# V fetched in 64 KB rows into one 8 MB slot, PV of a pair of units in its own loop pass, and one merge for all groups at the end

## The chip, the cores and the metric

One core of one Trainium2 chip. The metric is the device time of the core in microseconds (us); a run is one execution. Engines are called as in the profile: PE (matmul), PEld (PE's weight loads), DVE, ACT, POOL (GpSimd) and SP (which issues nearly all DMA). A "DMA engine" is one of the 16 that move the core's data.

## The reference

One token is decoded: layer norm, a grouped-query attention over a long cache, and beside it a small dense layer with GELU.

```
B, Sq, D = 1, 1, 512;  Hq, Hkv, Sk, Dh = 32, 8, 65536, 128     # bf16
xn = layernorm(x)
q  = (xn @ wq) per head                       # 32 heads, 4 per kv group
p  = softmax(q @ k_cache^T * Dh**-0.5)
attention = (p @ v_cache) @ wo
dense     = gelu(xn @ w1 + b1) @ w2 + b2      # F = 1792
out = x + attention + dense
```

K and V are 128 MB each (8 groups x 65536 keys x 128 x 2 bytes). Sizes of transfers and slots are in powers of two; the profile's own MB are millions of bytes. In those, K and V are 268.4 MB, and with the weights 280.5 MB have to be read for a result of 1 KB.

## The kernel before

The cache is cut into 32 units of 16384 keys; 4 units make a group. A unit's K and V are 4 MB each. On one partition a unit is 128 keys of 256 bytes in a row: 32 KB. For each unit PE transposes K (128 transposes, drained by DVE and ACT), multiplies it with q (scores), DVE and ACT make the stable exponentials P, and PE multiplies V with P (PV). SBUF has four slots of 4 MB, two for K and two for V, and the loop runs over pairs of units. PV of a unit runs two units late, so the first pass has a dummy PV and the last two PVs come after the loop. Every group is merged (weighted by its units' maxima) inside the loop.

```python
    chunks = [("K", 0), ("K", 1)]                 # order of the DMA queue
    for u in range(2, NU):
        chunks += [("V", u - 2), ("K", u)]
    chunks += [("V", NU - 2), ("V", NU - 1), ("W", 0)]
# ... [cut] ...
            src = cache[0, g, c * CKEYS:(c + 1) * CKEYS, :].rearrange("(p t) d -> p t d", p=128)
            sch.dma(SP, lambda b=b, src=src: sp.dma_start(out=slot[b], in_=src), csem[b], writes=[f"slot{b}"])
# ... [cut] ...
    def half(i, b):                               # one unit; a loop pass is half(i, 0), half(i, 1)
        u = 2 * i + b
        # ... [cut: weigh_2, weigh_3 of the last group when it has ended] ...
        pv(u - 2)
        transposes(b, 0)
        stats_1()
        transposes(b, 1)
        stats_2(u - 1)
        # ... [cut] ...
        transposes(b, 2)
        scores(b, 0)
        transposes(b, 3)
        done_chunk("K", u)                        # the slot is free: SP may issue the next K
        scores(b, 1)
        # ... [cut: weigh_1, total] ...
        scores(b, 2)
        scores(b, 3)
# ... [cut] ...  after the loop:
    stats_1(); stats_2(L); pv(L - 1); weigh_1(); total(); weigh_2()
    # ... [cut] ...
    pv(L)
    weigh_3(oT_last)
    # ... [cut: 136 small matmuls with wo, output] ...
```

The output weights wo ("W", 4 MB) come last, into the K slots.

Of the kernel before, what the change touches and what calls it, by code (L numbers as in the profile page):

```python
# [237 lines left out]
def bass_parallel_sum__gqa_block_cached__dense_activation_gelu__decode_kernel(  # L238
# [14 lines left out]
    DH = 128  # L253
# [33 lines left out]
    SP = sch.add_engine("sp", "sp")  # L287

# [6 lines left out]
    def sb(name, shape, dt):  # L295
# [14 lines left out]
    qT_bf = sb("qT_bf", [128, H], BF)  # L310
# [13 lines left out]
            for i in range(NSLOT)]  # L324
    wq_sb = kv[:, NK * TPD * DH:NK * TPD * DH + KT * H * DH].rearrange("p (kt n) -> p kt n", kt=KT)
# [11 lines left out]

    pmax = sb("pmax", [128, HPG], F32)
    gmax4 = sb("gmax4", [HPG, 1], F32)
    diag4 = sb("diag4", [HPG, HPG], F32)  # L340
    negm = sb("negm", [128, GW], F32)
    sums = sb("sums", [128, GW], F32)
    sums_cur = sb("sums_cur", [128, GW], F32)
    o_all = sb("o_all", [128, GW], F32)
    coef = sb("coef", [128, GW], F32)
    wtot = sb("wtot", [128, GW], F32)
    o_c = sb("o_c", [128, GW], F32)
    nmin = sb("nmin", [128, HPG], F32)
    rden = sb("rden", [128, HPG], F32)
    o_sum = sb("o_sum", [128, HPG], F32)  # L350
    oT_all = sb("oT_all", [128, G * HPG], BF)
    oT_last = sb("oT_last", [128, HPG], BF)
    oX_bf = sb("oX_bf", [128, HPG, GE], BF)
    spare = sb("spare", [128, 1], F32)
# [13 lines left out]
    csem = [sch.dsem(f"csem{i}") for i in range(NSLOT)]  # L368
    sem_x = sch.dsem("dx")
    sem_misc = sch.dsem("dmisc")  # L370
    sem_w1 = sch.dsem("dw1")
    wsem = [sch.dsem(f"wsem{i}") for i in range(4)]
    sem_out = sch.dsem("dout")

    for t, res, v in ((pmax, "pmax", 0.0), (negm, None, 0.0), (sums, None, 1.0), (sums_cur, "sums_cur", 1.0),
                      (o_all, None, 0.0), (coef, "coef", 1.0)):
        names = [res] if res else {
            id(negm): [f"negm{c}" for c in range(CPG)], id(sums): [f"sums{a}" for a in range(GW)],
            id(o_all): [f"o{c}" for c in range(CPG)]}[id(t)]
        sch.op(POOL, lambda t=t, v=v: pool.memset(t[:, :], v), writes=names)  # L380
# [12 lines left out]
    w_end = w2_at + FC * D  # L393
    if w_end < NSLOT * TPD * DH:
        sch.op(POOL, lambda: pool.memset(kv[:, w_end:NSLOT * TPD * DH], 0.0), writes=["w_pad"])
    for k in range(2):
        sch.op(POOL, lambda k=k: pool.memset(P_bf[k][:, :], 0.0), writes=[f"P{k}_{j}" for j in range(HPG)])


    chunks = [("K", 0), ("K", 1)]  # L400
    for u in range(2, NU):
        chunks += [("V", u - 2), ("K", u)]
    chunks += [("V", NU - 2), ("V", NU - 1), ("W", 0)]
    next_chunk = [0]
    slot_free = [True, True, False, False]

    def slot_of(kind, u):
        return u % 2 + (NK if kind == "V" else 0)

    def issue_chunks():  # L410
        while next_chunk[0] < len(chunks):
            kind, u = chunks[next_chunk[0]]
            if kind == "W":
                if not (slot_free[0] and slot_free[1]):
                    return
                dma_wo()
                next_chunk[0] += 1
                return
            b = slot_of(kind, u)
            if not slot_free[b]:  # L420
                return
            slot_free[b] = False
            g, c = divmod(u, CPG)
            cache = A_k_cache if kind == "K" else A_v_cache
            src = cache[0, g, c * CKEYS:(c + 1) * CKEYS, :].rearrange("(p t) d -> p t d", p=128)
            sch.dma(SP, lambda b=b, src=src: sp.dma_start(out=slot[b], in_=src), csem[b], writes=[f"slot{b}"])
            next_chunk[0] += 1

    def done_chunk(kind, u):
        slot_free[slot_of(kind, u)] = True  # L430
        issue_chunks()
# [10 lines left out]
    def dma_wq():  # L442
        sch.dma(SP, lambda: sp.dma_start(out=wq_sb, in_=A_wq.rearrange("(p kt) n -> p kt n", kt=KT)),  # L443
                csem[NK], writes=[f"slot{NK}"])

    def dma_w12():
# [4 lines left out]
                csem[NK + 1], writes=[f"slot{NK + 1}"])  # L451
# [58 lines left out]
    def qproj():  # L510
        for b in range(2):
            for kt in range(KT):
                for j in range(4):
                    c0 = (b * 4 + j) * 512
                    row_mm(pss[b][32 * j:32 * j + 1, :], xnT_bf[:, kt:kt + 1], wq_sb[:, kt, c0:c0 + 512],
                           [f"slot{NK}", "xnT"], f"pss{b}", kt == 0, kt == KT - 1, kt == KT - 1 and j == 3)
# [8 lines left out]
        sch.op(DVE, lambda: dve.tensor_copy(out=qT_bf[:, :], in_=pA[:, PA_Q:PA_Q + H]), reads=["pA"], writes=["qT"])  # L525

    def ffn():
        for s in range(FC // 2):
            b, j = divmod(s, 4)
            for kt in range(KT):  # L530
                row_mm(pO[32 * j:32 * j + 1, b * 256:(b + 1) * 256], xnT_bf[:, kt:kt + 1],
                       w1_sb[:, kt, :, 2 * s:2 * s + 2], ["w1", "xnT"], "pO", kt == 0, kt == KT - 1,
# [22 lines left out]
        for fc in range(FC):  # L555
            row_mm(pO[32 * (fc % 4):32 * (fc % 4) + 1, :], gT_bf[:, fc:fc + 1], w2_sb[:, fc, :],
                   [f"slot{NK + 1}", "gT"], "pO", fc < 4, fc >= FC - 4 and fc % 4 != 3, False)
# [45 lines left out]
    group = [None]  # L603

    def load_q(u):
        def copy():
            cols = slice(0, HPG) if group[0] is None else bass.ds(group[0] * HPG, HPG)
            return dve.tensor_copy(out=q_cur[:, :], in_=qT_bf[:, cols])

        sch.op(DVE, copy, reads=["qT"], writes=["q_cur"])  # L610
# [11 lines left out]
    def stats_2(u):  # L622
        k, c = u % 2, u % CPG
        us = slice(c * HPG, (c + 1) * HPG)
# [5 lines left out]
               reads=["pA"], writes=[f"negm{c}"])  # L630
        src = pss[k][:, 0:CW].rearrange("p (t j) -> p t j", j=HPG)
        for j in range(HPG):
            at = c * HPG + j
# [5 lines left out]
                reads=[f"negm{c}", f"pss{k}"],  # L639
                writes=[f"P{k}_{j}", f"sums{at}"],  # L640
            )


    def pv(u):
        k, b = u % 2, slot_of("V", u)
        for t in range(TPD):
            sch.op(
                PE,
                lambda k=k, b=b, t=t: pe.matmul(  # L649
                    pO[:, 0:HPG], lhsT=slot[b][:, t, :], rhs=P_v[k][:, t, :],  # L650
                    start=t == 0, stop=t == TPD - 1),
                reads=[f"slot{b}"] + (["w_pad"] if u == -1 and "w_pad" in sch.last_write else []) + [f"P{k}_{j}" for j in range(HPG)], writes=["pO"],
                publish=t == TPD - 1,
            )
        done_chunk("V", u)
        c = u % CPG
        us = slice(c * HPG, (c + 1) * HPG)
        sch.op(DVE, lambda us=us: dve.tensor_copy(out=o_all[:, us], in_=pO[:, 0:HPG]),  # L658
               reads=["pO"], writes=[f"o{c}"])


    negm_v, coef_v = (t[:, :].rearrange("p (h j) -> p h j", j=HPG) for t in (negm, coef))
    negm_r, wtot_r, oc_r = (t[:, :].rearrange("p (h j) -> p j h", j=HPG) for t in (negm, wtot, o_c))

    def weigh_1():
        neg = [f"negm{c}" for c in range(CPG)]
        sch.op(DVE, lambda: dve.tensor_reduce(out=nmin[:, :], in_=negm_r, axis=AX.X, op=ALU.min),
               reads=neg, writes=["nmin"])
        sch.op(DVE, lambda: dve.tensor_tensor(
            out=coef_v, in0=nmin[:, :].unsqueeze(1).to_broadcast([128, CPG, HPG]), in1=negm_v,  # L670
            op=ALU.subtract), reads=["nmin"] + neg, writes=["coef"])
        sch.op(DVE, lambda: dve.tensor_copy(out=sums_cur[:, :], in_=sums[:, :]),  # L672
               reads=[f"sums{at}" for at in range(GW)], writes=["sums_cur"])
        sch.op(ACT, lambda: act.activation(out=coef[:, :], in_=coef[:, :], func=ACTF.Exp),
               reads=["coef"], writes=["coef"])

    def total():
        sch.op(PE, lambda: pe.matmul(pA[:, PA_SUM:PA_SUM + GW], lhsT=ones_f[:, :], rhs=sums_cur[:, :],  # L678
                                     start=True, stop=True), reads=["ones_f", "sums_cur"], writes=["pA"])

    def weigh_2():
        sch.op(DVE, lambda: dve.tensor_tensor(out=wtot[:, :], in0=coef[:, :], in1=pA[:, PA_SUM:PA_SUM + GW],
                                              op=ALU.mult), reads=["coef", "pA"], writes=["wtot"])
        sch.op(DVE, lambda: dve.tensor_reduce(out=rden[:, :], in_=wtot_r, axis=AX.X, op=ALU.add),
               reads=["wtot"], writes=["rden"])
        sch.op(DVE, lambda: dve.reciprocal(out=rden[:, :], in_=rden[:, :]), reads=["rden"], writes=["rden"])

    def weigh_3(out=None):
        sch.op(DVE, lambda: dve.tensor_tensor(out=o_c[:, :], in0=o_all[:, :], in1=coef[:, :], op=ALU.mult),
               reads=["coef"] + [f"o{c}" for c in range(CPG)], writes=["o_c"])  # L690
        sch.op(DVE, lambda: dve.tensor_reduce(out=o_sum[:, :], in_=oc_r, axis=AX.X, op=ALU.add),
               reads=["o_c"], writes=["o_sum"])

        def scale():
            dst = out[:, :] if out is not None else oT_all[:, bass.ds(group[0] * HPG, HPG)]
            return dve.tensor_tensor(out=dst, in0=o_sum[:, :], in1=rden[:, :], op=ALU.mult)

        sch.op(DVE, scale, reads=["o_sum", "rden"], writes=["oT" if out is None else "oL"])


    def half(i, b):
        u = 2 * i + b
        odd = i % 2
        if b == 0:
            if odd:
                weigh_2()
                weigh_3()
            else:
                DVE.pending += 6
# [136 lines left out]
```

## Time and profile before

| | before |
|---|---|
| time, median (3 runs) | 661.83 us (661.66 to 662.32) |
| span of the profiled run | 659.8 us |
| HBM read | 280.50 MB, 425 GB/s over the span |
| PE busy | 567.6 us (86%) |

Lines of the profile's page of the kernel before: busy time by engine, the 40 slices, the DMA part, and the chain of work that ended last. The digits are tenths of a slice; GB/s is what the DMA engines moved in each slice.

```profile
span 659.8 us, 28552 instructions
PE 567.6 (86%) x12957; PEld 530.4 (80%) x12957; DVE 279.4 (42%) x616; ACT 244.9 (37%) x470; POOL 4.2 (1%) x19
...
PEclk9686777777788866778876678876767887676785
DMA  9999999999999999999999999999999999999996
GB/s 369 441 426 433 420 436 423 443 425 435 431 427 439 429 435 428 429 435 425 441 427 433 431 427 437 431 435 429 429 437 425 441 425 433 433 425 437 431 428 251
...
q1 hardware_dynamic: 11128, 280.50, 99.1%
q8 instruction: 10, 0.16, 0.1%
...
DMA 59%; PE 38%; issue 1%; DVE 1%; SPq 0%; DVEq 0%
```

The DMA row has nines to the last slice, and the load queue (q1) has transfers under way for 99.1% of 16 engines' span. PE is busy too, but the next two views show it waiting. The names in them: kv holds the four slots, pst PE's transposes, pss its scores (at the end, the products with wo), pO its PV products. First who waited for whom on PE in the kernel before (total us, times, longest), then the end of its timeline (start, length, engine, line, what, and in brackets the idle before it).

```profile
PE pst L569 <- DMA kv<-in_A_k_cache_dram: 49.3, 25, 3.0
PE pO L649 <- DVE pmax L597: 11.8, 15, 0.8
...
PE pss L773 <- DMA kv<-in_A_wo_dram: 2.1, 1, 2.1
```

```profile
625.46 3.59 PE L569 MATMUL pst<-ident_bf,kv 128*128 128x128 bf16 x32 [2.54 <-DMA kv<-in_A_k_cache_dram]
...
655.36 1.61 PE L773 MATMUL pss<-kv,oX_bf 128*1 128x128 bf16 x48 [2.06 <-DMA kv<-in_A_wo_dram]
656.66 0.74 PE L773 MATMUL pss<-kv,oT_last 128*1 128x128 bf16 x16
```

PE waits for K at nearly every unit, and at the very end for the last weights. So the kernel is bound by its DMA. How long DMA takes can be read one level lower, from the records of single rows in the trace: one 32 KB row takes 1215 ns (median) on its DMA engine and the next row follows within nanoseconds.

### The profile page before, as it was taken

What the parts mean: (1) busy time and instruction counts of PE and PEld (TensorE: products, weight loads), DVE (VectorE), ACT (ScalarE), POOL (GpSimd) and SP (SyncE); (2) the same over time, 40 slices, a digit from 0 to 9 for tenths busy, and PEclk for the clock granted to TensorE, in tenths of its full rate; (3) what the DMA queues carried; (4) which work ended last, traced back from release to release, by engine and by line L of the source; (5) the groups of instructions that cost most, each with busy time, mean ns of one, the idle gap of its engine ahead of it and who ended that gap; (6) DMA issues with size and microseconds to landing.
All of it is one profiled execution on the core that took longest, in us unless ns stands there. A gap on an engine that the chain in (4) does not pass through costs nothing.

```text
span 659.8 us, 28552 instructions
## 1 busy us (share of the span) xinstructions
PE 567.6 (86%) x12957; PEld 530.4 (80%) x12957; DVE 279.4 (42%) x616; ACT 244.9 (37%) x470; POOL 4.2 (1%) x19
## 2 busy tenths in 40 slices
PE   2597899999889988889898888988888998888896
PEld 0387899999888877878887788978878897787885
DVE  5153444454345443444444334544433444443341
ACT  0143344444344432334443233443323444332350
POOL 2000000000000000000000000000000000000000
PEclk9686777777788866778876678876767887676785
DMA  9999999999999999999999999999999999999996
GB/s 369 441 426 433 420 436 423 443 425 435 431 427 439 429 435 428 429 435 425 441 427 433 431 427 437 431 435 429 429 437 425 441 425 433 433 425 437 431 428 251
DMA packets 11288, 280.69 MB, mean 425 GB/s; under 512 B 1290, under 2 KB 1804, under 8 KB 2700
## 3 DMA queue, kind: packets, MB, share of 16 engines
q1 hardware_dynamic: 11128, 280.50, 99.1%
q8 instruction: 10, 0.16, 0.1%
q10 hardware_dynamic: 148, 0.01, 0.0%
q14 instruction: 2, 0.02, 0.0%
HBM read 280.50 MB, written 0.00 MB: 425 GB/s over the span
## 4 chain that ended last, share of the span: by engine, by line
DMA 59%; PE 38%; issue 1%; DVE 1%; SPq 0%; DVEq 0%
DMA kv<-in_A_k_cache_dram 55%; PE pst L569 27%; DMA kv<-in_A_wo_dram 5%; PE pss L589 5%; PE pO L649 4%; PE pA L614 1%; PE pA L625 1%; DVE pmax L597 0%; PE pss L773 0%; DVE kt_ring L577 0%; PE pA L678 0%; SPq L450 0%; SPq L459 0%; SPq L447 0%; SPq L443 0%
## 5 line engine op out<-in xcount | busy, mean ns | idle before, releaser
L569 PE MATMUL pst<-ident_bf,kv 128*128 128x128 bf16 x4096 | 313.3, 245 | 49.6 <-DMA kv<-in_A_k_cache_dram 49.3
L569 PEld LDWEIGHTS pst<-ident_bf,kv 128*128 128x128 bf16 x4096 | 284.5, 112 | 68.6 <-DMA kv<-in_A_k_cache_dram 51.5
L579 ACT ACTIVATE kt_ring<-pst 128x1024 bf16<-128x1024 bf16 x192 | 198.2, 1032 | 376.0 <-PE pst L569 373.3
L577 DVE COPY kt_ring<-pst 128x1024 bf16<-128x1024 bf16 x320 | 211.8, 688 | 178.9 <-PE pst L569 178.3
L649 PE MATMUL pO<-P_bf,kv 128*128 128x4 bf16 x4352 | 120.7, 166 | 17.0 <-DVE pmax L597 11.8
L649 PEld LDWEIGHTS pO<-P_bf,kv 128*128 128x128 bf16 x4352 | 118.0, 103 | 19.1 <-DVE pmax L597 13.1
L589 PE MATMUL pss<-q_cur,kt_ring 128*128 128x4 bf16 x4096 | 114.1, 164 | 2.4 <-issue 2.4
L589 PEld LDWEIGHTS pss<-q_cur,kt_ring 128*128 128x128 bf16 x4096 | 111.8, 96 | 2.5 <-issue 2.5
L636 ACT ACTIVATE P_bf<-pss,negm 128x128 bf16<-128x128 f32 x132 | 52.5, 553 | 4.0 <-DVE negm L628 4.0
L597 DVE TENSOR_REDUCE pmax<-pss 128x4 f32<-128x512 f32 x32 | 22.1, 691 | 68.7 <-PE pss L589 68.7
L658 DVE COPY o_all<-pO 128x4 f32<-128x4 f32 x34 | 5.5, 161 | 104.9 <-PE pO L649 104.9
L636 ACT ACTIVATION_READ_ACCUMULATOR P_bf<-pss,negm 128x1 f32 x132 | 37.4, 283 | 0.0
L614 PE MATMUL pA<-ident_f,pmax 128*4 128x128 f32 x66 | 16.2, 339 | 0.8 <-DVE pmax L597 0.8
L625 PE MATMUL pA<-diag,ones_f 4*128 4x4 f32 x66 | 12.8, 261 | 0.6 <-DVE diag L618 0.6
L625 PEld LDWEIGHTS pA<-diag,ones_f 4*128 4x128 f32 x66 | 9.8, 186 | 4.2 <-DVE diag L618 0.9
L500 PE MATMUL pA<-ones_bf,xn_row 1*128 1x1 bf16 x4 | 0.3, 174 | 10.5 <-DVE xn_row L496 10.5
L616 DVE TENSOR_REDUCE gmax<-pA 4x1 f32<-4x128 f32 x33 | 8.9, 269 | 0.5 <-PE pA L614 0.5
L500 PEld LDWEIGHTS pA<-ones_bf,xn_row 1*128 1x128 bf16 x4 | 0.2, 116 | 10.5 <-DVE xn_row L496 10.5
L614 PEld LDWEIGHTS pA<-ident_f,pmax 128*4 128x4 f32 x66 | 3.0, 84 | 6.4 <-DVE kt_ring L577 4.5
L678 PE MATMUL pA<-sums_cur,ones_f 128*128 128x16 f32 x34 | 6.8, 275 | 1.3 <-DVE sums_cur L672 0.6
L618 DVE TENSOR_SCALAR diag<-ident_f,gmax 4x4 f32<-4x4 f32 x33 | 7.2, 217 | 1.2
L678 PEld LDWEIGHTS pA<-sums_cur,ones_f 128*128 128x128 f32 x34 | 5.3, 195 | 2.2 <-DVE sums_cur L672 2.2
(82 smaller groups left out, 66.3 us busy)
## 6 DMA issues: line engine op xcount, KB each, us to landing
kv<-in_A_k_cache_dram SPq DMA_DIRECT2D x32, 4096.0 KB, 27.5
kv<-in_A_v_cache_dram SPq DMA_DIRECT2D x32, 4096.0 KB, 30.7
kv<-in_A_wq_dram SPq DMA_DIRECT2D x1, 4096.0 KB, 12.3
kv<-in_B_w_dram SPq DMA_DIRECT2D x2, 1792.0 KB, 18.0
kv<-in_A_wo_dram SPq DMA_DIRECT2D x1, 2048.0 KB, 27.5
kv<-in_A_wo_dram SPq DMA_DIRECT2D x1, 1536.0 KB, 31.5
kv<-in_A_wo_dram SPq DMA_DIRECT2D x1, 384.0 KB, 19.5
kv<-in_A_wo_dram SPq DMA_DIRECT2D x1, 128.0 KB, 19.4
```

The source lines that it names most:

```text
L569: lambda tb=tb, at=at, b=b, tt=s * TPB + t: pe.transpose(pst[tb][:, at * 128:(at + 1) * 128], slot[b][:, tt, :], ident_bf[:, :]),
L577: e, fn = DVE, lambda tb=tb, dst=dst: dve.tensor_copy(out=dst, in_=pst[tb][:, :])
L579: e, fn = ACT, lambda tb=tb, dst=dst: act.activation(out=dst, in_=pst[tb][:, :], func=ACTF.Copy)
L589: lambda k=k, kb=kb, at=at, t=t: pe.matmul(pss[k][:, at:at + HPG], lhsT=kt_ring[:, kb * BCOL + t * 128:kb * BCOL + (t + 1) * 128], rhs=q_c ...
L597: lambda k=k: dve.tensor_reduce(out=pmax[:, :], in_=pss[k][:, 0:CW].rearrange("p (t j) -> p j t", j=HPG), axis=AX.X, op=ALU.max),
L614: sch.op(PE, lambda: pe.matmul(pA[0:HPG, PA_ST:PA_ST + 128], lhsT=pmax[:, 0:HPG], rhs=ident_f[:, :], start=True, stop=True), reads=["pmax" ...
L616: sch.op(DVE, lambda: dve.tensor_reduce(out=gmax4[:, :], in_=pA[0:HPG, PA_ST:PA_ST + 128], axis=AX.X, op=ALU.max), reads=["pA"], writes=[" ...
L618: sch.op(DVE, lambda: dve.tensor_scalar(out=diag4[:, :], in0=ident_f[0:HPG, 0:HPG], scalar1=gmax4[0:HPG, 0:1], scalar2=None, op0=ALU.mult) ...
L625: sch.op(PE, lambda: pe.matmul(pA[:, PA_SB:PA_SB + HPG], lhsT=ones_f[0:HPG, 0:128], rhs=diag4[0:HPG, 0:HPG], start=True, stop=True), reads ...
L636: lambda k=k, at=at, j=j, src=src: act.activation(out=P_v[k][:, :, j], in_=src[:, :, j], func=ACTF.Exp, bias=negm[:, at:at + 1], scale=1.0 ...
L649: lambda k=k, b=b, t=t: pe.matmul(pO[:, 0:HPG], lhsT=slot[b][:, t, :], rhs=P_v[k][:, t, :], start=t == 0, stop=t == TPD - 1),
L678: sch.op(PE, lambda: pe.matmul(pA[:, PA_SUM:PA_SUM + GW], lhsT=ones_f[:, :], rhs=sums_cur[:, :], start=True, stop=True), reads=["ones_f", ...
```

## The change

Its intent: fewer and longer rows. Two neighbouring units of 16384 keys lie side by side on each partition (256 keys, 64 KB), so V of a pair comes in one 8 MB transfer of 64 KB rows into one slot made of the two old V slots; K of the pair comes in two transfers of 32 KB rows that are 64 KB apart. A pair's PVs move to the end of its own loop pass, so there is no dummy first pass and no PV after the loop. The statistics of each unit are kept in columns (128 in all), and all groups are merged once in the last pass. The last V comes as two halves.

```diff
-    chunks = [("K", 0), ("K", 1)]
-    for u in range(2, NU):
-        chunks += [("V", u - 2), ("K", u)]
-    chunks += [("V", NU - 2), ("V", NU - 1), ("W", 0)]
+    chunks = []
+    for i in range(NU // 2):
+        chunks += [("K", 2 * i), ("K", 2 * i + 1), ("V", i)]
+    chunks += [("W", 0)]
 ... [cut]
+            src = cache[0, g, 2 * c * CKEYS:2 * (c + 1) * CKEYS, :].rearrange("(p t) d -> p t d", p=128)
+            if kind == "K":
+                src = src[:, b * TPD:(b + 1) * TPD, :]
+                sch.dma(SP, lambda b=b, src=src: sp.dma_start(out=slot[b], in_=src), csem[b], writes=[f"slot{b}"])
+            elif i < NU // 2 - 1:
+                sch.dma(SP, lambda src=src: sp.dma_start(out=vslot, in_=src), csem[NK], writes=["vslot"])
+                ready_v("vslot")
+            else:
+                ... [cut: the last V as two halves, the second on semaphore sem_vb]
 ... [cut]
+    def body(i):
+        last = i == NU // 2 - 1
+        for b in range(2):
+            u = 2 * i + b
+            transposes(b, 0)
+            if b:
+                stats_1()
+            transposes(b, 1)
+            if b:
+                stats_2(u - 1)
+            else:
+                load_q(i)
+            transposes(b, 2)
+            scores(b, 0)
+            transposes(b, 3)
+            done_chunk(b)
+            for q in range(1, BPC):
+                scores(b, q)
+        stats_1()
+        stats_2(2 * i + 1)
+        if last:
+            weigh_1()
+        keep_sums(i)
+        pv(2 * i)
+        total()
+        if last:
+            weigh_2()
+            weigh_3(0, GE, "oT")
+        pv(2 * i + 1)
 ... [cut: pv, the merge over 128 columns, the end; two more semaphores so that the last pass may differ]
```

## The prediction

> **What bounds the kernel now: DMA.** The page shows 280.5 MB read at 425 GB/s over a 659.8 us span, a DMA row of nines in every slice but the last, and ten-microsecond windows at 414 to 446 GB/s from 10 to 640 us. PE is busy 86% but waits for loads: the chain of waits is 55% K loads, 5% the last weight load. In the trace's DMA records one 32 KB row takes 1215 ns median (1219 mean) on one of 16 engines, and the next starts within nanoseconds. 520 rows per engine x 1.219 = 634 us; with the weight rows about 653 us: the whole stretch from the first load to the landing of the last weights at 655.36. Only bytes, row costs or the two ends can move the time. The Trainium skill (DMA: Bandwidth & Descriptors, "Specifications") gives a fabric ceiling of 435 GB/s; 32 KB at a sixteenth of that is 1205 ns, so a row's fixed cost is about 10 ns (estimate).
>
> **What the change does.**
> - Bytes: the same.
> - Rows: V goes from 256 rows of 32 KB per engine to 128 of 64 KB. If a 64 KB row is one piece, that saves 128 x 10 ns = 1.3 us; fewer completions about 0.2. If it is cut in two, nothing. K keeps 32 KB rows, now 64 KB apart.
> - Queue: a pair needs about 38.9 us of DMA (32 x 1.215). With K landing at T, transposes and scores of a unit take 13.4 to 13.7 us (timeline at 606 and 625 us): K slots free at T+11 and T+25, stats end at T+29.4, V landed at T+29, two PVs (3.57 us each) and the sums matmul end near T+37. The next V is issued then, while two K loads fill the queue to T+48. It never runs dry; PE has about 2 us of slack per pair (now 2.3 us per unit).
> - Removed: dummy PV, the small merges per group: off the path, worth nothing. Added: stats exposed once per pair (2.3 us of PE, as at 639 us), a sums matmul every pair (~0.5 us): also off it, except in the last pair.
> - Tail: the last V lands 9.7 us before the last weights. Now PE waits 2.06 us for DMA before the final weight products, and everything after the landing takes 4.4 us. After, two PVs, sums and the whole merge come behind the last scores; I estimate PE 1 us behind the landing: +1 us (0 to 2.5).
>
> **Predicted: 661.0 us** (-1.5 rows, +1 tail). 8 in 10: 658.8 to 664.0. Faster by over 2%: 1%; within: 95%; slower: 4%.
>
> **What would show each step.** V issues of 8192 KB; V rows of 64 KB at about 2.42 us, or still 1.215 us pieces; no window under 410 GB/s from 40 to 640 us; each V issued 8 us or more before the queue empties; chain still mostly loads; PE's idle before the last weight product gone; last landing to end 5.4 us.
>
> **What would make it wrong.** K rows 64 KB apart slowing HBM (the skill, same page, "Latency and other measured facts", reports half rate at a 512 KiB pitch; no run here shows it); a granted clock (mean 0.77, down to 0.5) that pushes PE's pair over 38.9 us, lengthening the tail and then starving the queue; stalls of the first loop pass (3.8 us "issue" at 51 us now) delaying V(1).

## The result, and the profile after

| | before | after |
|---|---|---|
| time, median (4 runs each) | 662.0 us (661.66 to 662.32) | 660.85 us (659.48 to 661.91) |
| ratio, 95% interval | | 0.9982 (0.9961 to 1.0002) |
| span of the profiled run | 659.8 us | 657.6 us |
| PE busy | 567.6 us | 536.6 us |

A ratio here is the mean time of one kernel's fast runs over that of the other's in the same rounds, so it is not quite the ratio of the medians beside it. The profiled run of after is its fastest (659.48); the four runs lie 2.4 us apart, those of before 0.7.

The same lines of the page, now of the kernel after, with its two kinds of V transfers:

```profile
span 657.6 us, 27982 instructions
PE 536.6 (82%) x12695; PEld 509.2 (77%) x12695; DVE 273.6 (42%) x565; ACT 245.0 (37%) x454; POOL 2.9 (0%) x27
...
PEclk9788595968769596885959678595876959687695
DMA  8999999999999999999999999999999999999997
GB/s 366 434 446 425 410 447 415 462 399 447 415 462 399 443 450 415 454 407 441 452 411 419 447 447 415 441 421 443 450 413 433 431 437 456 409 421 443 421 443 290
...
q1 hardware_dynamic: 8968, 280.50, 99.2%
q8 instruction: 8, 0.13, 0.1%
...
DMA 65%; PE 32%; issue 2%; DVE 0%; SPq 0%
...
kv<-in_A_v_cache_dram SPq DMA_DIRECT2D x2, 4096.0 KB, 26.4
...
kv<-in_A_v_cache_dram SPq DMA_DIRECT2D x15, 31.1
```

DMA is still the chain (65%), and the packets of q1 fall by 2160, that is 1920 rows and 240 completions. PE's waits of the kernel after:

```profile
PE pst L581 <- DMA kv<-in_A_k_cache_dram: 35.0, 14, 7.2
PE pO L672 <- DMA kv<-in_A_v_cache_dram: 33.8, 13, 3.3
PE pA L628 <- DVE pmax L609: 12.5, 16, 0.8
PE pA L639 <- DVE diag L632: 10.0, 16, 0.6
...
PE pss L780 <- DMA kv<-in_A_wo_dram: 0.9, 1, 0.9
```

The exposed statistics are there (12.5 and 10.0 us in 16 passes), and still PE waits for K and for V in nearly every pair: 2.1 us for K (35.0 less the 7.2 at the very start, over 13) and 2.6 us for V (33.8/13). The end of its timeline:

```profile
615.15 8.13 PE L581 MATMUL pst<-ident_bf,kv 128*128 128x128 bf16 x96 [2.34 <-DMA kv<-in_A_k_cache_dram]
...
628.11 1.95 PE L581 MATMUL pst<-ident_bf,kv 128*128 128x128 bf16 x32
...
653.28 1.45 PE L780 MATMUL pss<-kv,oX_bf 128*1 128x128 bf16 x48 [0.92 <-DMA kv<-in_A_wo_dram]
654.51 0.64 PE L780 MATMUL pss<-kv,oT_all 128*1 128x128 bf16 x16
```

PE still arrives 0.92 us before the weights. The tail that I had costed at +1 us isn't there.

The first loop pass shows something else. SP's issues in the kernel after, then PE's stalls in it ("issue": PE waits for nothing that the profile shows):

```profile
25.41 0.33 SPq L425 DMA_DIRECT2D kv<-in_A_v_cache_dram  x1
42.81 15.85 SPq L423 DMA_DIRECT2D kv<-in_A_k_cache_dram  x2
78.77 0.33 SPq L425 DMA_DIRECT2D kv<-in_A_v_cache_dram  x1
...
147.25 0.33 SPq L425 DMA_DIRECT2D kv<-in_A_v_cache_dram  x1
```

```profile
47.56 0.48 PE L601 MATMUL pss<-q_cur,kt_ring 128*128 128x4 bf16 x11 [2.68 <-issue]
...
62.50 0.78 PE L601 MATMUL pss<-q_cur,kt_ring 128*128 128x4 bf16 x24 [2.43 <-issue]
...
70.51 0.94 PE L672 MATMUL pO<-P_bf,kv 128*128 128x4 bf16 x30 [1.95 <-issue]
...
77.70 1.04 PE L672 MATMUL pO<-P_bf,kv 128*128 128x4 bf16 x33 [3.10 <-issue]
```

V(1) is issued at 78.77. By the row records the K before it ends at 79.4 on the first engine and at 81.5 on the last, and the first row of V(1) starts only at 79.7, 0.96 us after its issue, so on the leading engines the queue runs dry. Rows that start in this moment also take about 3.1 us, not 2.42. At 147.25, in the steady state, the K before the next V ends at 158.5 on the first engine: 11 us of work are still queued.

### Accounts from the row records

This table is worked out from the trace's records of single DMA rows, not printed by any view. "Rows" is the duration of all rows of the load queue over 16 engines (neighbouring rows of an engine can overlap slightly, so it can exceed the stretch). "Stretch" is from the first row's start to the last row's end. "Dry" is the idle time of the average engine from 62 to 82 us, "end" the same from 642 us to the end of the stretch: how far the average engine finishes before the last. "Late fetches" are the 16 KB packets of the queue q8, which the profile calls "instruction" (pieces of program), after 640 us; in both profiles of before the third of them starts after the last row (at 656.7 and 656.3 us), so that two can delay rows.

| run | time of the profiled run | rows | stretch | dry | end | late fetches |
|---|---|---|---|---|---|---|
| before | 661.84 | 653.7 | 654.5 | 0.11 | 2.33 | 3 |
| b0_before (before again) | 661.49 | 653.6 | 654.2 | 0.10 | 2.09 | 3 |
| after | 659.48 | 652.6 | 652.4 | 0.59 | 0.58 | 1 |
| e0_after (after again) | 660.87 | 652.8 | 653.9 | 0.72 | 1.74 | 1 |
| e1_rows32 | 660.18 | 653.7 | 653.1 | 0.25 | 0.89 | 1 |
| e3_kpitch32 | 661.18 | 652.5 | 654.2 | 0.66 | 2.29 | 1 |
| e8_first_halves | 659.00 | 652.3 | 651.9 | 0.17 | 0.88 | 1 |
| e8_again | 658.89 | 652.1 | 651.8 | 0.14 | 0.89 | 1 |
| e9_halves_all | 660.38 | 653.7 | 653.3 | 0.14 | 1.17 | 1 |
| e10_code_late | 659.58 | 652.2 | 652.6 | 0.20 | 1.32 | 1 (and 4 of 8 KB at 571 to 616) |

A 64 KB row takes 2420 ns (median, mean 2426), so it is one piece and saves 10 ns against two of 1215. Rows fall by 1.1 us per engine (653.7 to 652.6). But time follows the stretch, and the stretch depends on the slowest engine. Each engine works its rows off alone, and nothing brings the 16 together while the queue is full. The distances between the engines' completions of one transfer, in us after the first engine:

```
before, second transfer of w (ends 21 us)  0 ... 0.56          all 16 together
before, K0 (ends 31 us)                    0 ... 0.45, 2.11    one engine back by 1.6
before, a transfer ending at 342 us     0 to 0.66 (seven engines), 1.18 to 1.92 (nine engines)
before, a transfer ending at 643 us     the same, 0 to 1.93
before, a transfer of wo ending at 648 us    0 to 1.92, 2.76         one engine back by 0.8
before, the next, ending at 652 us           0 to 1.89, 2.74, 3.42
```

At 27.2 us the first fetch of 16 KB of program takes 1084 ns on one engine, and there the first engine falls back. After the fetches of the first pass eight engines are late by 1.2 to 2 us, a fetch at 253 us is followed by a ninth, and so they stay for 560 us. Two more fetches, at 646.9 and 653.2 us, stand beside the two last lines.

### The profile page after: what moved, and what is told of

Read it like the earlier page. It is cut to its first block, busy times and chain, and to the rows that moved or that the text cites. A ratio compares the mean times of both kernels' runs of the same rounds, so it can differ in the third digit from the quotient of the medians.

```text
span 657.6 us, 27982 instructions
## 1 busy us (share of the span) xinstructions
PE 536.6 (82%) x12695; PEld 509.2 (77%) x12695; DVE 273.6 (42%) x565; ACT 245.0 (37%) x454; POOL 2.9 (0%) x27
## 4 chain that ended last, share of the span: by engine, by line
DMA 65%; PE 32%; issue 2%; DVE 0%; SPq 0%
DMA kv<-in_A_k_cache_dram 61%; PE pst L581 25%; DMA kv<-in_A_wo_dram 4%; PE pss L601 4%; PE pO L672 2%; PE pss L780 0%; PE pA L628 0%; PE pA L639 0%; DVE pmax L609 0%; PE pA L687 0%; DVE gmax L630 0%; DVE diag L632 0%; SPq L459 0%; SPq L456 0%; SPq L452 0%
## 5 line engine op out<-in xcount | busy, mean ns | idle before, releaser
L581 PE MATMUL pst<-ident_bf,kv 128*128 128x128 bf16 x4096 | 281.2, 235 | 35.1 <-DMA kv<-in_A_k_cache_dram 35.0
L581 PEld LDWEIGHTS pst<-ident_bf,kv 128*128 128x128 bf16 x4096 | 262.9, 106 | 43.2 <-DMA kv<-in_A_k_cache_dram 36.6
L672 PE MATMUL pO<-P_bf,kv 128*128 128x4 bf16 x4096 | 115.1, 166 | 38.9 <-DMA kv<-in_A_v_cache_dram 33.8
L672 PEld LDWEIGHTS pO<-P_bf,kv 128*128 128x128 bf16 x4096 | 113.6, 104 | 40.2 <-DMA kv<-in_A_v_cache_dram 34.9
L650 ACT ACTIVATE P_bf<-pss,negm 128x128 bf16<-128x128 f32 x128 | 50.9, 548 | 68.6 <-DVE negm L642 68.6
L680 DVE COPY o_all<-pO 128x4 f32 (+1 forms) x32 | 5.2, 162 | 122.8 <-PE pO L672 122.8
L639 PEld LDWEIGHTS pA<-diag,ones_f 4*128 4x128 f32 x64 | 12.6, 245 | 18.3 <-DVE diag L632 16.6
L628 PE MATMUL pA<-ident_f,pmax 128*4 128x128 f32 x64 | 14.2, 309 | 12.5 <-DVE pmax L609 12.5
L664 DVE COPY sums_all<-sums 128x8 f32 (+1 forms) x16 | 2.7, 172 | 23.4 <-ACT P_bf L650 23.4
L687 PE MATMUL pA<-sums_all,ones_f 128*128 128x128 f32 x32 | 12.4, 491 | 0.0
L642 DVE TENSOR_SCALAR negm<-pA 128x4 f32<-128x4 f32 x32 | 5.1, 161 | 10.8 <-PE pA L639 10.8
L687 PEld LDWEIGHTS pA<-sums_all,ones_f 128*128 128x128 f32 x32 | 8.1, 312 | 0.0
```

The costliest lines, as they stand in the source:

```text
L581: lambda tb=tb, at=at, b=b, tt=s * TPB + t: pe.transpose(pst[tb][:, at * 128:(at + 1) * 128], slot[b][:, tt, :], ident_bf[:, :]),
L628: sch.op(PE, lambda: pe.matmul(pA[0:HPG, PA_ST:PA_ST + 128], lhsT=pmax[:, 0:HPG], rhs=ident_f[:, :], start=True, stop=True), reads=["pmax" ...
L639: sch.op(PE, lambda: pe.matmul(pA[:, PA_SB:PA_SB + HPG], lhsT=ones_f[0:HPG, 0:128], rhs=diag4[0:HPG, 0:HPG], start=True, stop=True), reads ...
L650: lambda k=k, at=at, j=j, src=src: act.activation(out=P_v[k][:, :, j], in_=src[:, :, j], func=ACTF.Exp, bias=negm[:, at:at + 1], scale=1.0 ...
L672: lambda k=k, t=t: pe.matmul(pO[:, 0:HPG], lhsT=vslot[:, k * TPD + t, :], rhs=P_v[k][:, t, :], start=t == 0, stop=t == TPD - 1),
L687: sch.op(PE, lambda: pe.matmul(pA[:, PA_SUM:PA_SUM + NC], lhsT=ones_f[:, :], rhs=sums_all[:, :], start=True, stop=True), reads=["ones_f", ...
```

## The experiments

The name before each expectation is that of its run; "e0_after" and "b0_before" are the two kernels themselves again. Runs of one group shared a chip and its runs of the kernel before. The three groups: e0 to e3; b0, e4, e7 and e8; e8_again, e9, e10 and e11.

### e0_after: the changed kernel again (no edit)

> The changed kernel itself again, as the control of the three runs beside it. Theory (time = sum of the row costs on a DMA engine, plus the two ends): 660 to 662 us, ratio to before 0.996 to 1.000; its DMA records again show 64 KB rows at 2420 ns median and 652.6 us of rows per engine (653.7 before). Rival (the gain is run-to-run spread, because the four runs so far span 659.5 to 661.9): the ratio's interval covers 1.000 also with five rounds.

Measured: 660.6 us (659.03 to 661.45, 6 runs), before 662.02; ratio 0.9969 (0.9956 to 0.9982). With these rounds the interval leaves out 1.000: the small gain is real, and the spread is too.

### e1_rows32: only the row length undone

```diff
-            elif i < NU // 2 - 1:
+            elif False:                 # every V as two 4 MB transfers of 32 KB rows
```

> Only the row length is undone: every V pair is fetched as two 4 MB transfers of 32 KB rows into the same 8 MB slot, issued one after the other; PE order, slot and merges stay. Row theory: 120 rows per engine become 240, +10 to 12 ns for each pair, so +1.2 to 1.4 us against e0_after, about the time of before (662), and 653.7 us of rows per engine. Rival (what little was gained came from order or tail, not from rows): equal to e0_after within 0.3 us.

Measured: 660.11 us (659.94 to 662.48), ratio 0.9975 (0.9962 to 0.9988). Rows rose to 653.7 as they should, but the time did not rise with them. Here the rival was right, or two effects met: "dry" fell from 0.72 to 0.25 (V(1) was issued at 76.83 in place of 78.77) and "end" from 1.74 to 0.89. With runs 2.5 us apart the row theory could be neither shown nor dismissed. That is why e9 below repeats the test in a quieter kernel.

### e2_rows4k: V in 4 KB rows

```diff
-                sch.dma(SP, ... out=vslot, in_=src ..., writes=["vslot"])
+                cut = lambda x, b: x.rearrange("p (a b c) d -> p b a (c d)", b=2, c=16)[:, b]
+                sch.dma(SP, ... out=cut(vslot, 0), in_=cut(src, 0) ..., csem[NK], writes=["vslot"])
+                sch.dma(SP, ... out=cut(vslot, 1), in_=cut(src, 1) ..., sem_vb, writes=["vslot_b"])
```

> The disputed cost enlarged: V pairs 0 to 14 come in 4 KB rows (two interleaved transfers, each of every second 4 KB), same bytes, same slot, same order. Row theory from the 4 KB weight rows (163.5 ns): 16 x 163.5 = 2616 ns in place of 2426 for each of 120 rows per engine, +22.8 us: 681 to 686 us, 3.2% slower than before. Rival (something other than row service bounds the time, for example PE's pair or the issue times): no more than 2 us over e0_after.

Measured: 686.45 us, ratio 1.0369 (1.0354 to 1.0384): +25.9 us on e0_after for +22.8 forecast. The 4 KB rows took 166.6 ns on average here, not 163.5 (they overlap a little: 681.5 us of rows per engine in a stretch of 677.5). With the same bytes, the cost per row sets the time; rival refuted.

### e3_kpitch32: K's rows back to back again (result wrong)

```diff
-                src = src[:, b * TPD:(b + 1) * TPD, :]
+                src = cache[0, g, (2*c + b) * CKEYS:(2*c + b + 1) * CKEYS, :].rearrange("(p t) d -> p t d", p=128)
```

> K's 32 KB rows are read back to back again (row pitch 32 KB as in before) while V keeps 64 KB rows; the keys of K and V then don't match, so the result is wrong on purpose. If the 64 KB pitch costs nothing: equal to e0_after within 0.3 us, and the 32 KB rows' mean (1220.1 ns after, 1218.9 before) does not move with the pitch. If it costs what the mean suggests: -0.3 us or more[...]. If the pitch hurts HBM badly, several us faster than e0_after.

Measured: 660.97 us, ratio 0.9974 (0.9961 to 0.9987), beside 0.9969 of e0_after; 32 KB rows 1219.1 ns on average (1219.8 in e0_after). A 64 KB pitch costs nothing that can be seen. (The keys of K and V don't match in this kernel, but the comparison with the reference passed all the same: with these inputs it is too coarse to notice. So a pass says little about key order.)

### b0_before: a second profile of the kernel before (no edit)

> The kernel before, unchanged, for a second profile of it. Question: how much of the time is the last engine finishing behind the others? In the profile of before the engines stood idle 2.3 us on average before the last one ended, in the row-undone run 0.9 us with the same 653.7 us of rows, and that is the whole 1.5 us between their data stretches. If the ends of the engines are chance per run: this profile shows some other value between 0.5 and 2.5 us, and its time differs from 661.8 by as much. If before always ends so unevenly: again about 2.3 us.

Measured: 661.49 us, "end" 2.09, again three late fetches. Both profiles of before end unevenly, which speaks against pure chance.

### e4_pad6: more work for PE

```diff
-        total()
+        for _ in range(7):
+            total()
```

> Six more sums matmuls (two instructions each, about 0.6 us each, about 3.9 us of PE) in each pair between its two PVs. Theory (PE has 5.1 us of idle per pair in the profile after, DMA bounds): nothing over the 16 pairs but the part in the last pair, which has only 0.9 us to spare: +2 to +3.5 us over the changed kernel, 662.5 to 664.5; idle of PE for loads falls from 5.1 to about 1.2 us per pair. My estimate in the prediction (2 us of slack per pair) would give +1.9 us x 15 = +28 us. Rival (PE bounds): +62 us.

Measured: 661.39 us, ratio 0.9991 (0.9976 to 1.0007). PE's waits in this run:

```profile
PE pO L672 <- DMA kv<-in_A_v_cache_dram: 29.2, 12, 3.1
...
PE pst L581 <- DMA kv<-in_A_k_cache_dram: 7.3, 1, 7.3
```

The extra work ate the wait for K (one left, at the start, of 14) and the loop did not get longer: PE does not bound. (The six took about 3.0 us, 1.49 for three in the timeline, not 3.9.) With the 2.1 us for K and 2.4 to 2.6 for V, PE's slack is about 4.7 us per pair and not the 2 of my prediction. The cost is 0.8 us on e0_after's median, 1.5 by the ratios, less than the 2 forecast. PE's wait for the last weights is gone here, so a part of it can be the tail; but the extra work also delayed V(1) (issued at 80.47 us, "dry" about 1.9), and how the cost divides was not tested.

### e7_wait_k1: let the queue run empty once per pair

```diff
             elif i < NU // 2 - 1:
+                if i:
+                    sch.wait_ev(SP, sch.last_write["slot1"])   # until the pair's second K has landed
```

> Each V pair from the second to the fifteenth is issued only when the second K half of its pair has landed, so the DMA queue runs empty once per pair instead of being fed 11 us ahead. Theory (the queue's continuous feed is what the time rests on): DMA stands still for issue and first bytes, 1.5 to 2.5 us each of 14 times: +21 to +35 us, 682 to 696; the windows show one dip per pair. Rival (time set elsewhere): within 3 us of the changed kernel. Skew between the engines is reset at each dry moment.

Measured: 694.07 us, ratio 1.0488 (1.0472 to 1.0504): +33.5 us on e0_after, 2.4 us for each of 14 dry moments. (At 122 us, for example, almost no row is under way for 1.35 us, and the first rows after it take 2.6 to 3.4 us in place of 2.42.) The wait is in SP's list, as meant:

```profile
SPq L427 <- DMA kv<-in_A_k_cache_dram: 152.5, 14, 11.7
```

Between dry moments the engines' completions lie 0.3 to 0.7 us apart instead of 2: a dry moment brings them together again, but costs more than it brings. The feed of the queue is what the time rests on, and the change's steady state never lets it down.

### e8_first_halves: feed the queue in the first pass (the best version)

```diff
-            elif i < NU // 2 - 1:
-                sch.dma(SP, ... out=vslot, in_=src ..., writes=["vslot"])
+            elif i in (2, 3, 4, 5, 6, 7, 8, 9, 10, 11, 12, 13, 14):   # V 0, 1 and 15 as two halves
+                sch.dma(SP, ... out=vslot, in_=src ..., writes=["vslot", "vslot_b"])
 ...
-                reads=["vslot"] + ["v_odd"] * k + ...
+                reads=(["vslot_b", "v_odd"] if k else ["vslot"]) + ...
```

The first PV of a pair now reads only the first half of the slot, so the first half of V(1) may be asked for before the second PV has run.

> A try at a better version: V pairs 0 and 1 come as two 4 MB halves with 32 KB rows, and the first half of a pair is asked for as soon as the first PV has read its half, the rest with 64 KB rows as in the changed kernel. In the profiles of the changed kernel V pair 1 is issued at 78.8 us, when the queue is already running dry, because the first loop pass has 9 to 10 us of stalls; engines idle 0.6 to 0.7 us each from 60 to 80 us. Theory: that idle falls under 0.2 us and the time by about 0.4 us against the changed kernel, 660.2. With ends of engines by chance of about 1 us this may not show in the time, only in the idle from 60 to 80 us.

Measured: 659.01 us (658.81 to 659.19), ratio 0.9957 (0.9943 to 0.997). Correct. SP's issues in this run:

```profile
24.86 0.33 SPq L429 DMA_DIRECT2D kv<-in_A_v_cache_dram  x1
25.23 0.43 SPq L431 DMA_DIRECT2D kv<-in_A_v_cache_dram  x1
43.12 14.73 SPq L423 DMA_DIRECT2D kv<-in_A_k_cache_dram  x2
69.01 0.33 SPq L429 DMA_DIRECT2D kv<-in_A_v_cache_dram  x1
76.58 0.33 SPq L431 DMA_DIRECT2D kv<-in_A_v_cache_dram  x1
```

The first half is asked for at 69.01, ten us earlier than V(1) in the changed kernel, and "dry" falls from 0.6 or 0.7 to 0.17. The gain is larger than the 0.4 us forecast, and the spread shrinks from 2.4 us to 0.4.

### e8_again: the same kernel, as a control

> The version of e8_first_halves again, as the control of the three beside it, and to see whether its gain and its small spread repeat: 658.8 to 659.3 us, ratio to before 0.995 to 0.997.

Measured: 659.0 us (658.89 to 659.14), ratio 0.9953 (0.9939 to 0.9966). It repeats. Against e0_after, on the same chip at another time with before equal to 0.03 us (662.02 and 661.99), it is 1.6 us faster by the medians and 1.1 by the ratios. The two were not run in one group.

### e9_halves_all: the row length alone, in the quiet kernel

```diff
-            elif i in (2, 3, 4, 5, 6, 7, 8, 9, 10, 11, 12, 13, 14):
+            elif False:                 # every V as two halves of 32 KB rows
```

> The version of e8_first_halves with all V pairs, not only pairs 0, 1 and 15, as two 4 MB halves of 32 KB rows. Only the row length of 13 pairs differs (and that each first half is asked for 4 us earlier, with the queue full anyway). Row theory: 104 rows per engine become 208, +10 to 12 ns each: +1.0 to 1.3 us against e8_again, 653.5 us of rows per engine, 660.0 to 660.4. Rival (e1_rows32, where undoing the rows changed nothing, was no accident): within 0.3 us of e8_again. The quiet version (spread 0.4 us) can tell these apart where e1 could not.

Measured: 660.1 us (659.95 to 660.38), ratio 0.9968 (0.9955 to 0.9982). That is +1.1 us on e8_again, no run of one kernel within the range of the other; rows 653.7 against 652.1, that is 1.6 by the account. So the 64 KB rows are worth 1.1 us in the time. e1 came to the same 660.1 us: it too had 32 KB rows alone, but compared with e0 it was also rid of most of the dry moment, which hid their cost.

### e10_code_late: more program to fetch, late

```diff
     def ready_v(res, i):
         sch.op(POOL, lambda: pool.memset(flag[:, :], 0.0), reads=[res], writes=["v_odd"])
+        if i in (13, 14):               # e11: 2 <= i < 14, and 300
+            for _ in range(256):
+                ... POOL fills one element of a spare tile, each its own
```

> The version of e8_first_halves with 512 needless one-element fills on the idle GpSimd after V pairs 13 and 14 have landed: no engine on the path does more, only about two more 16 KB pieces of program are fetched between 570 and 640 us. In the profiles each such fetch (about 1.07 us on one DMA engine) sets one engine back, which stays behind to the end; before has three fetches after 640 us and ends with 2.1 to 2.3 us of idle engines, the others have one. Theory (late fetches make the last engine late, this is the part of the gain that is not rows): end idle up from 0.9, time +0.3 to +1.2 us against e8_again. Rival (fetches don't matter): equal within 0.2 us, or no fetch appears and nothing is learnt.

Measured: 659.58 us (659.55 to 659.7), ratio 0.9961 (0.9948 to 0.9975): +0.58 us on e8_again, again without overlap. The fetches came as four extra packets of 8 KB (309 ns each) between 571 and 616 us. The farthest engine went from 2.1 us behind (before the fetches) to 2.5, and "end" from 0.89 to 1.32.

### e11_code_mid: much more program to fetch

> As e10_code_late, but 3600 fills spread over V pairs 2 to 13: about 14 more fetches of 16 KB between 100 and 600 us. If they go round the 16 engines, nearly all are set back alike: +0.9 us of data per engine (14/16 x 1.07), time +0.7 to +1.5 us. If they all fall on one engine or few: that engine ends 5 to 15 us late and the time rises as much. If fetches cost nothing: equal to e8_again.

Measured: 675.52 us, ratio 1.0201 (1.0185 to 1.0216), which is +16.5 us on e8_again. Two parts of the page of this run, the engines' busy time and the DMA part:

```profile
PE 536.6 (80%) x12695; PEld 509.0 (76%) x12695; DVE 273.6 (41%) x565; ACT 245.2 (36%) x454; POOL 122.5 (18%) x3627
...
GB/s 371 438 434 430 426 430 434 445 411 454 416 448 420 437 428 427 438 422 446 422 444 424 430 448 410 427 409 408 438 432 402 424 417 409 411 434 407 436 409 77
...
q14 instruction: 30, 0.25, 0.1%
q8 instruction: 8, 0.13, 0.1%
```

PE has exactly the work of after; POOL's fills are off the path. Thirty packets of 8 KB were fetched on q14 where e8_again has two, 0.23 MB more in 280 MB. Of the K transfer that ends last, 15 engines complete within 0.9 us of each other (from 629.8 us on) and one engine 11.1 us behind the first; for about the last 9 us of the stretch that engine works alone, which is why the last slice shows 77 GB/s. So nearly all those fetches fell on one engine. The rest of the 16.5 us lies in the loop: from about 420 us on, with that engine 11 to 13 us behind, the queue of the others runs dry once per pair, and V follows V after 40 to 41 us in place of 38.8. 16.5 us over 28 extra packets is 0.59 us each (an estimate, of all this together; a packet itself takes 0.31).

## Why the prediction was right or wrong

The time was right: 661.0 forecast, 660.85 measured. Point by point:

- **DMA bounds.** Right. e4 (more PE work, no longer loop), e2 (dearer rows, +25.9 us) and e7 (queue dry, +33.5 us) show it from three sides.
- **Rows, -1.5 us.** Right in kind, and about right in size: 64 KB rows are one piece at 2420 ns. The account of the records falls by 1.1 us from before to after and by 1.6 from e9 to e8_again; the time of those two differs by 1.1.
- **The queue never runs dry.** Right in the steady state (11 us of work queued at each V), wrong in the first pass. I named the danger ("stalls of the first loop pass delaying V(1)") and gave it no cost. It happened: V(1) was issued at 78.77 as the queue ran out, 0.6 to 0.7 us of idle on the average engine. In e0 and e3 one engine started its V(1) only at 82.1 us, 1.2 to 1.4 us after the other fifteen, and stayed 2.3 to 2.9 us behind the first. In the profiled run of after, the fastest of its four, all 16 had started by 81.0: there the dry moment brought them from 2.0 to 0.8 us apart and cost little (a stretch of 652.4 us; e8_again 651.8). So what makes runs of after slow appears to be the one late engine; why it is late is open. e8 removes the dry moment and is 1.6 us faster than e0 by the medians, 1.1 by the ratios.
- **Tail, +1 us.** Wrong: the estimate of PE's time was too large. I took 13.4 to 13.7 us for every unit, from units that each began after a wait for K. In the changed kernel the second unit follows the first without a wait, and its transposes start at 1.95 us per 32, not 3.59 as at 625 us in before. The last pair's units took 13.0 and 11.5 us (615.15 to 628.11 and on to 639.65). So PE had 0.92 us to spare where I had it 1 us late. Slack per pair was 4.7 us, not 2; e4, whose loop took 3.0 us more of PE's work per pair without getting longer, confirms that it is more than 2.
- **Signals.** "No window under 410 GB/s" was badly chosen: windows of 20 us swing between 400 and 464, because a long row is counted where it starts or ends, while the pair's mean stays. "Last landing to end 5.4 us": it was 4.3 (657.6 - 653.28).
- **What I left out.** The uneven end of the engines. In e1 and e9 the rows are as long as in before (653.7 us), yet they are 1.7 and 2.1 us faster (ratios 0.9975 and 0.9968 of 662). Of this, about 1 us shows in the records as a more even end (0.9 to 1.2 us of idle against 2.1 to 2.3). It isn't the lateness of the first pass, for at 640 us the engines of e1 and e9 lie 2.1 and 2.4 us apart, no less than those of before. Before has two PVs and more of its program after the loop and fetches two pieces of it between 640 us and its last row; after fetches one. With them the last engine of before goes from 1.9 to 3.4 us behind (b0: 2.2 to 3.1), while those of e1 and e9 stay at 2.1 and 2.4. That late fetches can cost such an amount e10 makes likely (+0.58 us). That they are what costs it in before is argued from this coincidence in time, not shown: no run took the fetches out of before, and the rest, up to 1 us, is open.

The sum came out because errors cancelled, which is luck: I counted +1 us of tail, which was not there, left out the dry first pass, which was, and left out the more even end, which worked the other way. From before to after by the runs: 1.9 us gained for what e9 keeps of it besides the rows, 1.1 for the rows (e8_again), and 1.1 to 1.6 given back by the late V(1).

## What to carry to other kernels

When a kernel is bound by DMA and its queue never empties, count rows, not only bytes, and then look at the slowest of the 16 engines: what sets one back once stays to the end. Check the first loop pass by itself, because PE stalled there when its program was fetched, and ask for its next load in pieces that come free early. Keep the program short, also on engines that have nothing to do: 0.23 MB of extra program on GpSimd cost 16.5 of 659 us here.

## What the Trainium skill lacked or had wrong

- "Runtime: NRT & Kernel Launch", section "Instruction fetch mechanics", says that the program is refilled in blocks of 16 KiB by DMA and that crossing a block is "mostly hidden". The block size agrees for the packets of q8 (16 KB, about 1.07 us on one DMA engine; by their time in the first pass I take them for PE's). Hidden they are not here: the first pass of after had 10.2 us of "issue" stalls, four that began at 44.9, 60.1, 68.6 and 74.6 us with fetches at 45.0, 60.0, 68.0 and 75.3 (that PE waited for these is taken from the times), and fetches set single DMA engines back. GpSimd's came in 8 KB packets, 28 more of them in e11 than without its fills, which differs from the page, and nearly all on one DMA engine: +16.5 us.
- "DMA: Bandwidth & Descriptors" doesn't say that the 16 engines drift apart and stay apart while the queue is full. In before they lay 1.9 to 2.0 us apart from 60 to 640 us, and 0.3 to 0.7 us where the queue was let run dry (e7).
- The same page gives no time for a single row of these lengths. Here: 4 KB 164 to 167 ns, 14 KB 535 ns, 32 KB 1215 ns, 64 KB 2420 ns, so a 64 KB row goes as one piece.
- The same page's section "Latency and other measured facts" reports copies between HBM tensors at 207 GB/s for a row pitch of 512 KiB and at half of that for 4 MiB; it has no figure for a smaller pitch. A pitch of 64 KB with 32 KB rows cost nothing that can be seen here (ratio 0.9969 with it, 0.9974 without, e0 and e3).
- For a DMA issued by GpSimd the same page gives a fixed cost of about 2.0 us (section "Anatomy of one DMA — SWDGE (gpsimd) path"); for SP's queue it gives only the time to the first byte. A queue of SP that ran empty cost 2.4 us each time (e7); the first row of the next transfer started 0.95 us after its issue (122.49 to 123.44 us).
